# Attention into a gated feed-forward on one core: other SBUF places for TensorE's stationary operands

## The chip, the core and the metric

The kernel runs on one core of a Trainium2 chip. The time is that of the device for one execution, in microseconds (us); three runs of the kernel before gave 672.59 as their median (672.45 to 673.4).

## What is computed

Two attentions one after the other, and on their result a feed-forward with the gate h / (1 + exp(-1.702 h)):

```python
def sm_attn(qq, kk, vv):
    s = scale * np.matmul(qq, kk.transpose(0, 1, 3, 2))
    s = s - np.max(s, axis=-1, keepdims=True)
    a = np.exp(s)
    a = a / (np.sum(a, axis=-1, keepdims=True) + 1e-09)
    return np.matmul(a, vv)
p_packed = sm_attn(p, k, v)
out = sm_attn(q, p_packed, p_packed)
...
h = x @ w_in
g = h * (1.0 / (1.0 + np.exp(-1.702 * h)))
return (g @ w_out).astype(np.float32)
```

There are 8 batches, 8 heads, 576 positions, 64 numbers a head and 32 packed positions. x is the attention's output as 4,608 tokens of 512 numbers; w_in is 512 x 2048, w_out 2048 x 512. All is float32.

## The kernel before

**Stages.** The second attention is never multiplied out. Its probabilities a are kept, and the packed values times w_in give a matrix m for each batch and each 512 of the 2,048 inner columns (`m_mm`, L535); then h is m times a. Four steps carry nearly all of TensorE's time:

- `h_mm` (L687) makes 128 inner columns of h for 288 tokens with six matmuls. m is the stationary operand (128 columns), a the moving one (288 columns).
- `g_main`, `g_over`, `g_sum` (L716 to L769) take h through the gate on ScalarE and make sums of blocks of g on VectorE, for a product scheme with seven products of blocks. `g_upper` and `g_lower` (L776, L787) split the seven blocks into an upper and a lower part, the tile gs: 2 x 7 x 128 numbers a partition.
- `prod` (L851) is the product with w_out: a block of gs is stationary (128 columns), a block of Wa or Wb is moving (256 columns). Each of the seven products takes three matmuls (upper with upper, upper with lower, lower with upper), so a unit of 128 pairs of inner columns takes 21.
- `prod0` (L809) does the same for batch 0 without the scheme, with a moving operand of 512 columns.

Every matmul has a weight load of its own, which fetches the stationary operand. In the trace the weight load of the next matmul begins some 3 ns after the start of the matmul before it.

**What is where.** m, a, gs, Wa and Wb are tiles of the pool `wk` (L77). A pool gives each tag a stretch of SBUF, as many tiles as the tag has buffers, one after another in the order in which the tags are first used, each tile rounded up to a multiple of 32 bytes. There are four tiles each of Wa and Wb (`NU`, L70; tags by `kp % NU` in `w_tile`, L219), one for each of the four units u; so Wb3 serves all products of u = 3 with the Wb blocks, that is nine of the 21 matmuls of these units. The plain weights that are split into Wa and Wb lie in Wb's places first (`plain_w`, L226). All slices that the matmuls take begin at multiples of 128 bytes from their tile's start, so a tile's start modulo 128 is also that of its slices. In the program that is built these are:

| tile | role on TensorE | start modulo 128, before |
|---|---|---|
| gs (3 buffers, L781; one more in a place of m) | stationary | 0 (64 in m's place) |
| m (3, L565) | stationary | 64 |
| a (3, L657) | moving | 64 |
| Wa0 to Wa3 | moving | 64 |
| Wb0, Wb1, Wb2 | moving | 64 |
| Wb3 | moving | 0 |
| kqv, x (k, q, v, attention) | both | 64 |
| aT, PT | stationary | 0 |
| X, r, raw of w_out (aT's and r's places) | not read by TensorE | 0 |

**Order.** The order of all steps is written out by hand in the table `order` (L931 to L1731), and each engine runs its own instructions in that order. Two lines of it, with the products of one unit among the steps of another:

```python
        (prod, 1, 7, 0, 0, "C"), (g_lower, 1, 7, 0, 1), (h_mm, 1, 7, 1, 0, 0), (g_main, 1, 7, 0, 3),
        (g_lower, 1, 7, 0, 2), (g_over, 1, 7, 0, 3), (prod, 1, 7, 0, 1, "D"), (h_mm, 1, 7, 1, 0, 1),
```

Of the kernel before, what the change touches and what calls it, by code (L numbers as in the profile page):

```python
# [8 lines left out]
F32 = mybir.dt.float32  # L9
# [12 lines left out]
def kernel(  # L22
# [33 lines left out]
    P = 128  # L56
    D = P // 2
    DM, DF = w_in.shape
    NP = DM // P
    B = q.shape[0]  # L60
    S = q.shape[2] // NP
    NPK = pk.shape[2] // NP - S
    NH = S // 2
    G = S // NPK
    FC = 512
    HC = FC // 2
    CF = FC // P
    KC = (S + P - 1) // P
# [4 lines left out]
    ABUFS, XBUFS, GBUFS, RBUFS = 3, 3, 3, 2  # L73
# [3 lines left out]
    wk = ctx.enter_context(tc.tile_pool(name="wk", bufs=1))  # L77
    ps_acc = ctx.enter_context(tc.tile_pool(name="ps_acc", bufs=1, space=PSUM))
    ps_h = ctx.enter_context(tc.tile_pool(name="ps_h", bufs=2, space=PSUM))
    dram = ctx.enter_context(tc.tile_pool(name="dram", bufs=1, space=bass.MemoryType.DRAM))  # L80

    ident = cst.tile([P, P], F32, name="ident")
    make_identity(nc, ident)
# [84 lines left out]
    raw = {}  # L168
# [1604 lines left out]
```

## Time and profile before

| | us |
|---|---|
| median of three runs | 672.59 (672.45 to 673.4) |
| profiled execution, from its first to its last instruction | 672.0 |
| TensorE, matmuls | 658.8 |
| TensorE, weight loads | 598.2 |
| VectorE | 555.0 |
| ScalarE | 409.3 |

The page gives no time of the profiled execution other than that span. Busy times are unions of what an engine's instructions cover. A matmul's own duration holds its way through the array, and the next one starts before it ends; what a matmul costs in a dense stream is the time from its start to the next one's start. It can be read from the timeline: the rows there merge matmuls of one kind that follow each other, with the start of the first, and the start of the row below ends the stretch.

### The profile page before, as it was taken

The page shows a single profiled execution, that of the slowest core. Times are in us where ns is not written, and L with a number is a line of the kernel's source. Part 1 is how long each engine was busy: PE and PEld are TensorE (multiplying, and loading weights), DVE is VectorE, ACT ScalarE, POOL GpSimd, SP SyncE. Part 2 cuts the span into 40 slices and gives each one's busy share as a digit, 9 for nine tenths or more (in the row PEclk, how much of TensorE's full clock was granted, in tenths as well). Part 3 has the DMA queues.
Part 4 walks back from the last instruction along what each step waited for, and adds up shares of the span by engine and source line. Part 5 has one row for each costly group of instructions (what it writes and reads, how often), then busy time and mean ns, then how long its engine had stood idle before and what let it go on. Part 6 is the DMA issues. An engine that isn't in the chain of part 4 may idle for free.

```text
span 672.0 us, 15271 instructions
## 1 busy us (share of the span) xinstructions
PE 658.8 (98%) x6227; PEld 598.2 (89%) x6227; DVE 555.0 (83%) x1132; ACT 409.3 (61%) x738; POOL 5.4 (1%) x15
## 2 busy tenths in 40 slices
PE   8999899999999999999999999999999999999996
PEld 6777698988989899898999799999999999999996
DVE  3969988879799796987999846878898878886897
ACT  5878777858677695886978554444443544434441
POOL 2100000000000000000000000000000000000000
PEclk9999999999999999999999999999999999999999
DMA  9885646745465476463785315141252222233221
GB/s 342 306 283 182 228 95 222 200 166 217 110 243 144 163 232 188 156 182 137 259 292 187 128 36 155 54 173 50 82 180 88 87 88 87 62 112 87 87 88 63
DMA packets 59174, 104.92 MB, mean 156 GB/s; under 512 B 31392, under 2 KB 36128, under 8 KB 58208
## 3 DMA queue, kind: packets, MB, share of 16 engines
q1 hardware_dynamic: 58960, 103.81, 47.3%
q8 instruction: 49, 0.80, 0.5%
q14 instruction: 21, 0.17, 0.1%
q10 hardware_dynamic: 144, 0.13, 0.1%
HBM read 70.51 MB, written 33.42 MB: 155 GB/s over the span
## 4 chain that ended last, share of the span: by engine, by line
PE 79%; DMA 7%; DVE 7%; ACT 4%; SPq 2%; issue 1%; DVEq 0%; ACTq 0%
PE h L699 25%; PE accC L860 11%; PE accA L860 11%; PE accB L860 10%; PE accD L860 6%; PE psm_None L547 4%; DMA raw_in_None<-w_in 2%; PE accA_over L860 2%; PE accB_over L860 2%; DMA home_m<-w_in 1%; PE accC_over L860 1%; PE ps L591 1%; DMA aT<-aside 1%; PE pspv_None L496 1%; DMA home<-w_in 1%; PE accD L816 1%
## 5 line engine op out<-in xcount | busy, mean ns | idle before, releaser
L699 PE MATMUL h<-a,m 128*128 128x288 f32 x1536 | 223.8, 296 | 2.5 <-ACT x L111 1.3
L699 PEld LDWEIGHTS h<-a,m 128*128 128x128 f32 x1536 | 208.2, 188 | 8.2 <-ACT x L111 2.9
L111 ACT CAST gs<-X 128x896 fp32r<-128x896 f32 (+2 forms) x117 | 104.6, 902 | 75.8 <-DVE X L769 17.8
L789 DVE TENSOR_TENSOR gs<-X,gs 128x896 fp32r<-128x896 f32 x112 | 120.8, 1086 | 22.8 <-ACT gs L111 22.3
L719 ACT ACTIVATE X<-h 128x512 f32<-128x512 f32 (+1 forms) x129 | 76.1, 597 | 83.4 <-PE h L699 77.7
L769 DVE TENSOR_TENSOR X<-X 128x256 f32<-128x256 f32 (+1 forms) x336 | 104.6, 330 | 21.6 <-ACT X L719 17.2
L860 PE MATMUL accC<-Wa,gs 128*128 128x256 f32 x672 | 98.1, 281 | 0.0
L860 PE MATMUL accB<-Wb,gs 128*128 128x256 f32 x672 | 97.7, 281 | 0.0
L860 PEld LDWEIGHTS accC<-Wa,gs 128*128 128x128 f32 x672 | 87.3, 188 | 5.2 <-issue 4.3
L860 PEld LDWEIGHTS accB<-Wb,gs 128*128 128x128 f32 x672 | 87.3, 188 | 1.9 <-issue 0.9
L860 PE MATMUL accA<-Wa,gs 128*128 128x256 f32 x336 | 59.0, 284 | 0.0
L860 PE MATMUL accD<-Wa,gs 128*128 128x256 f32 x336 | 58.5, 282 | 0.0
L860 PE MATMUL accA<-Wb,gs 128*128 128x256 f32 x336 | 57.8, 280 | 0.0
L860 PEld LDWEIGHTS accA<-Wa,gs 128*128 128x128 f32 x336 | 47.7, 188 | 5.4 <-issue 5.1
L860 PEld LDWEIGHTS accD<-Wa,gs 128*128 128x128 f32 x336 | 48.0, 188 | 4.6 <-issue 2.2
L111 ACT CAST m<-psm_None 128x1024 fp32r<-128x1024 f32 x31 | 30.8, 1016 | 29.4 <-PE psm_None L547 29.0
L860 PEld LDWEIGHTS accA<-Wb,gs 128*128 128x128 f32 x336 | 47.5, 188 | 0.0
L571 DVE TENSOR_TENSOR m<-psm_None,m 128x1024 fp32r<-128x1024 f32 x31 | 37.3, 1217 | 6.7 <-ACT m L111 6.5
L725 ACT ACTIVATE over<-h 128x64 f32<-128x64 f32 x128 | 35.3, 289 | 0.0
L547 PE MATMUL psm_None<-w_in,PT 64*32 64x512 f32 x496 | 32.6, 596 | 0.8 <-DVE x L601 0.8
L665 DVE TENSOR_TENSOR a<-xt,a 128x576 fp32r<-128x576 f32 x31 | 23.1, 745 | 2.5 <-ACT a L111 2.1
L719 ACT ACT_TABLE_LOAD x17 | 21.8, 1283 | 4.3 <-PE h L699 3.0
(203 smaller groups left out, 794.4 us busy)
## 6 DMA issues: line engine op xcount, KB each, us to landing
part<-r SPq DMA_DIRECT2D x14, 896.0 KB, 5.4
p<-part SPq DMA_DIRECT2D x14, 896.0 KB, 5.5
q<-q SPq DMA_DIRECT2D x16, 576.0 KB, 5.4
o<-r SPq DMA_DIRECT2D x16, 512.0 KB, 3.5
raw_out_None<-w_out SPq DMA_DIRECT2D x16, 511.8 KB, 5.6
v<-v SPq DMA_DIRECT2D x7, 1024.0 KB, 5.6
raw_in_None<-w_in SPq DMA_DIRECT2D x12, 511.8 KB, 4.8
k<-pk SPq DMA_DIRECT2D x8, 640.0 KB, 4.0
```

Of the source, the lines that this page charges most:

```text
L111: nc.scalar.copy(dst, src)
L496: nc.tensor.matmul(bank[32 * j : 32 * j + 32, e, e * D : (e + 1) * D], turned()[:, c, e, 32 * j : 32 * j + 32], vt[:, c, e0 : e0 + D], sta ...
L547: nc.tensor.matmul(banks[eo][32 * j : 32 * j + 32], PT[rows(eo), j, :], w_in_sb[c % 2][rows(eo), j, at], start=True, stop=True,)
L571: nc.vector.tensor_tensor(m[:, 1, :, at], st["bank", "m", b, c, part], m[:, 0, :, at].bitcast(F32), op=ALU.subtract,)
L591: nc.tensor.matmul(bank[32 * j : 32 * j + 32, eo, :NH], st["PT", b][rows(eo), j, :], kq["q0", half][rows(eo), j, :] if b == 0 else kq["q", ...
L665: engine.tensor_tensor(even_odd(a[:, 1], eo), even_odd(st["t", 2, b, half], eo), even_odd(a[:, 0], eo).bitcast(F32), op=ALU.subtract,)
L699: nc.tensor.matmul(h, m[:, part, eo, at], a[:, ap, eo * NH : (eo + 1) * NH], start=(n == 0), stop=(n == len(terms) - 1), skip_group_check= ...
L719: nc.scalar.activation(X[:, :4].rearrange("p (f t) n -> p f (t n)", f=2)[:, chunks(f)], st["h", *k][:, chunks(f), :NM], AF.Gelu_apprx_sigm ...
L725: nc.scalar.activation(over_part(ph, b, half, u), st["h", ph, b, half, u][:, :, NM:NH], AF.Gelu_apprx_sigmoid, scale=2.0,)
L769: engine.tensor_tensor(to, a, b_, op=ALU.subtract)
L789: engine.tensor_tensor(lo, X, hi.bitcast(F32), op=ALU.subtract)
L860: nc.tensor.matmul(acc[:, n * HC : (n + 1) * HC], gs[:, gp, g], Wa[:, wp, w] if w < 4 else Wb[:, wp, w - 4], start=(u == 0 and n == 0 and ...
```

## The change

At the pool's start a tile of each of the pool's tags is made, in a new order of the tags, with four tags that nothing else uses (`pad1` to `pad4`, of 32 or 96 bytes). No instruction touches these tiles; the kernel's own tiles then take the same stretches. Each engine's instructions, their order and the semaphores that they wait for and set are the same as before. Only addresses differ.

```diff
     dram = ctx.enter_context(tc.tile_pool(name="dram", bufs=1, space=bass.MemoryType.DRAM))
+
+    places = (
+        ("mx1", 2, 2), ("nb1", 2, 2), ("sm1", 2, 2), ("again", 1, 2), ("rs1", 1, 4), ("rsa", 1, 2),
+        ("mx2", G, 2), ("sm2", G, 2), ("rs2", G, 2),
+        ("kqv", KC * DM, 2), ("x", S, 6), ("Wb2", 6 * HC, 1), ("pad1", 8, 1),
+        ("gs", 14 * P, GBUFS), ("pad2", 24, 1), ("aT", KC * 2 * P, 1), ("X", 8 * P, XBUFS),
+        ("r", 7 * HC, 2), ("pn", 2 * D, 1), ("PT", P, 8), ("Wb3", 6 * HC, 1), ("raw", 2 * FC, RBUFS),
+        ("Wb0", 6 * HC, 1), ("pad3", 8, 1), ("m", 4 * FC, 3), ("pad4", 24, 1),
+    )
+    for tag, words, bufs in places:
+        for i in range(bufs if words else 0):
+            wk.tile([P, words], F32, tag=tag, name=f"place_{tag}_{i}", bufs=bufs)
 
     ident = cst.tile([P, P], F32, name="ident")
```

The starts that result, modulo 128:

| tile | before | changed |
|---|---|---|
| gs | 0 (64 in m's place) | 96 (also in m's place) |
| m | 64 | 96 |
| a, Wa0 to Wa3, Wb0 to Wb2, kqv, x | 64 | 64 |
| Wb3 | 0 | 64 |
| aT, PT, X, r | 0 | 64 |

The first weights of w_in, which are loaded into places of gs and of m at the program's start (`raw_tile`, L174), move with these.

## Rows read from the trace of the kernel before

**Rows 1.** The page: its first line, and busy time by engine (share, instructions).

```profile
span 672.0 us, 15271 instructions
PE 658.8 (98%) x6227; PEld 598.2 (89%) x6227; DVE 555.0 (83%) x1132; ACT 409.3 (61%) x738; POOL 5.4 (1%) x15
```

**Rows 2.** The page: granted TensorE clock in 40 slices, tenths of full speed.

```profile
PEclk9999999999999999999999999999999999999999
```

**Rows 3.** The page: chain that ended last, share of the span by engine.

```profile
PE 79%; DMA 7%; DVE 7%; ACT 4%; SPq 2%; issue 1%; DVEq 0%; ACTq 0%
```

**Rows 4.** Waits of TensorE, longest: us in total, times, longest us.

```profile
PE accD_warm L119 <- POOL ident masks.py:199: 1.4, 1, 1.4
```

**Rows 5.** Costly groups: line engine op, shapes, count | busy us, mean ns | idle before.

```profile
L699 PE MATMUL h<-a,m 128*128 128x288 f32 x1536 | 223.8, 296 | 2.5 <-ACT x L111 1.3 <-ACT over L725 1.0
...
L860 PE MATMUL accC<-Wa,gs 128*128 128x256 f32 x672 | 98.1, 281 | 0.0
...
L816 PE MATMUL accC<-Wa,gs 128*128 128x512 f32 x48 | 13.1, 404 | 0.0
...
L860 PE MATMUL accA_over<-Wb,gs_over 128*128 128x256 f32 x48 | 8.2, 280 | 0.0
```

**Rows 6.** Windows: length, each engine's busy us (count), PEclk, DMA share, GB/s.

```profile
415.07:419.15 4.08, 4.08 (x37) 4.08 (x36) 3.56 (x9) 2.66 (x5) 0.00 (x0) 1.00 0.96 308
257.23:262.05 4.82, 4.82 (x43) 4.82 (x42) 1.75 (x7) 1.51 (x3) 0.00 (x0) 1.00 0.74 274
```

**Rows 7.** Timeline of TensorE from 415.07: start us, us covered, operation, count.

```profile
415.07 0.50 PE L860 MATMUL accD<-Wa,gs 128*128 128x256 f32 x3
...
419.15 0.43 PE L699 MATMUL h<-a,m 128*128 128x288 f32 x2
```

**Rows 8.** Timeline of TensorE from 257.23, first and last start taken.

```profile
257.23 0.87 PE L860 MATMUL accC<-Wa,gs 128*128 128x256 f32 x6
...
261.82 0.51 PE L860 MATMUL accD<-Wa,gs 128*128 128x256 f32 x3
```

**Rows 9.** Timeline of TensorE: two stretches of nine products with Wb3, then what follows.

```profile
356.15 0.53 PE L860 MATMUL accA<-Wb,gs 128*128 128x256 f32 x3
...
357.24 0.52 PE L860 MATMUL accC<-Wa,gs 128*128 128x256 f32 x3
...
287.16 0.52 PE L860 MATMUL accA<-Wb,gs 128*128 128x256 f32 x3
...
288.23 0.56 PE L699 MATMUL h<-a,m 128*128 128x288 f32 x3
```

**Rows 10.** Timeline of TensorE: three long stretches of h, and what follows each.

```profile
591.17 4.91 PE L699 MATMUL h<-a,m 128*128 128x288 f32 x36
595.92 0.52 PE L860 MATMUL accB<-Wb,gs 128*128 128x256 f32 x3
...
322.57 3.29 PE L699 MATMUL h<-a,m 128*128 128x288 f32 x24
325.69 0.40 PE L860 MATMUL accD<-Wa,gs 128*128 128x256 f32 x2
...
580.49 3.39 PE L699 MATMUL h<-a,m 128*128 128x288 f32 x24
583.71 0.51 PE L860 MATMUL accD<-Wa,gs 128*128 128x256 f32 x3
```

**Rows 11.** Two of VectorE's lines: durations ns min/median/max, first and last start us.

```profile
L276 DVE TENSOR_TENSOR T<-E x16: 416/418/426, 57.3 to 376.2; 128x256 f32<-128x256 f32 x16
...
L789 DVE TENSOR_TENSOR gs<-X,gs x112: 1030/1086/1095, 81.7 to 651.0; 128x896 fp32r<-128x896 f32 x112
```

**Rows 12.** DMA issues into places of gs and of m: KB each, median us to landing.

```profile
home<-w_in SPq DMA_DIRECT2D x4, 255.8 KB, 7.5
home_m<-w_in SPq DMA_DIRECT2D x4, 255.8 KB, 6.7
```

## The prediction

> **What bounds the kernel now.** I read the page's head first. TensorE's matmuls cover 658.8 of the 672.0 us, VectorE follows with 555.0 and ScalarE with 409.3 [rows 1]. The granted clock is 9 tenths or more in every slice, the higher of its two levels (2.4 GHz), so no stretch is long because of the clock [rows 2]. The chain of waits that ended last runs for 79% on TensorE, with 7% each for DMA and VectorE [rows 3]. TensorE's own longest wait is 1.4 us, before the first matmul [rows 4]. So after the start-up the time is the number of matmuls times their pitch, the time from one start to the next, and the only thing that the change can do to the end is to alter that pitch, or to make another engine so slow that TensorE waits.
>
> The costly groups give the numbers [rows 5]: 1,536 matmuls of 288 columns (h, stationary m, moving a); 2,688 of 256 columns in ten groups (the products, stationary gs, moving Wa or Wb; the first and the last group are shown); 192 of 512 columns in four groups (first shown). The durations in these rows overlap (the next weight load runs during each matmul), so I don't use them. The pitch comes from the timeline.
>
> Two stretches show that the pitch isn't fixed. From 415.07 us, 36 products in a row take 4.08 us: 113.3 ns each [rows 7]. From 257.23 us, 39 products in nine rows take 4.59 us: 117.7 ns [rows 8]. Both have gs at 0 and Wa or Wb at 64 modulo 128 bytes. The windows tell that the load of the other engines isn't the reason: the **faster** stretch has VectorE busy 3.56 of 4.08 us and the DMA engines at 0.96, the slower one 1.75 of 4.82 and 0.74 [rows 6]. So one and the same pair of places has two pitches, and what the slow one pays, 4.4 ns a matmul, looks like something that happens between the two reads of TensorE itself: the weight load of the next matmul and the moving operand of this one.
>
> The places do matter, but less. Before the change one buffer breaks the pattern: Wb3 lies at 0, where gs also lies. Nine products with it take 1.09 us from 356.15 (121.1 ns), nine 1.07 us from 287.16 (118.9 ns) [rows 9]: 120.0 on the mean, 2.3 more than 117.7. For h, both operands lie at 64, also a distance of 0. Its stretches stand at 131.9, 130.0 and 134.2 ns [rows 10].
>
> **The change part by part.** Instructions, order and waits stay; only distances change. The distance from the moving to the stationary operand, modulo 128, becomes 32 for all three kinds. It was 64 for 2,400 of the products and for the 192 wide matmuls, 0 for the 288 products with Wb3 (9 in each of 32 units) and 0 for h.
>
> 1. Products with Wb3, 288: the distance 0 goes. I take the pitch of the other products: 288 x (120.0 - 117.7) = -0.7 us. Bounds: 0 if the place had no part in it; -1.9 us at 113.3 (288 x 6.7).
>
> 2. h, 1,536: the distance 0 goes too. No stretch shows h at another distance. The bounds are its own extremes: from 131.9 down to 130.0 is -2.9 us, up to 134.2 is +3.5 us. I take half of the way down, -0.95 ns, which is under half of the 2.3 ns that the products show between the distances 0 and 64: -1.5 us. I don't take all 2.3, because h shows no surplus over the products: its 32 more columns cost 131.9 - 117.7 = 14.2 ns, and 32 columns at 117.7 / 256 ns would be 14.7.
>
> 3. Products at 64, 2,400: to 32. This is the largest number and the one that the trace shows least. Bounds: all at 113.3 is -10.6 us; all at the slowest stretch with Wb3, 121.1, is +8.2 us. I take 0: long stretches at different buffers and different times sit at 117.7, so the slow pitch is a stable state that arises at most starts, and nothing in the rows says that 32 leaves it. The 192 wide ones I cost at 0 as well, for the same reason; at 4.4 ns either way they are 0.8 us.
>
> 4. The writers of the moved tiles. VectorE's sums of 256 elements take 416 to 426 ns with a median of 418 over tiles at 0 and at 64 [rows 11], so these two places cost it the same; 96 isn't shown. If each of the 112 lower parts of g (1,086 ns) [rows 11] grew by as much as that row's spread, 10 ns, VectorE would have 1.1 us more in a span where it idles 117 us. I cost it at nothing; TensorE's stream is the cover, and if it were gone the bound is that 1.1 us. The transfers into the gs places took 7.5 us at 0, into the m places 6.7 us at 64 [rows 12]; these wait in queues behind one another, so I read no effect of the place from the difference. They matter in the first 30 us only: 0, with 0.8 us either way.
>
> Sum: -0.7 - 1.5 = -2.2 us on a span of 672.0, so 669.8. The median of the runs, 672.59, is 0.6 us above that span (the page gives no other time for its execution), so the forecast is 670.4 us.
>
> The rows show two pitches at equal places [rows 7, 8] and a third, 2.3 ns longer, at another place [rows 9]. Against the whole change stands a rule of the Trainium skill: TensorE: Matmul & The Clock Gate, in Step-by-step: what each phase is for, says that TensorE reads SBUF through two independent ports and that loading the next weights takes no read bandwidth from the running matmul; by it the sum is 0 and the time stays 672.6. The equal places agree with it in so far as the place isn't all, the 2.3 ns speak against it. The same page, in Back-to-back issue gap, gives columns / 2.4 + 2.5 ns for an isolated matmul, 109.2 for 256 columns (an estimate from its formula); no stretch here gets there, the best is 113.3.
>
> **The rivals.** *The fast pitch becomes the rule.* If the distance 32 keeps the two reads from meeting, all products go to 113.3: 10.6 + 1.9 us. h would go to 113.3 + 14.2 = 127.5, another 1,536 x 4.4 = 6.8 us, and the wide ones 0.8: 20.1 us. VectorE would then be close behind in its dense stretches, so I keep three quarters: 15 us, 657 us. For it: the state exists, for 36 products on end and under more load. Against it: no row has the distance 32, and the state is rare.
>
> *The new distance is worse.* The reads meet more often, as they seem to with Wb3. If all products go to 121.1 and h to 134.2, that is 8.2 + 0.3 + 3.5 = +12.0 us, 684.6; half-way, 678.6. It decides as soon as the 2,400 products lose 0.9 ns on the mean, which eats the 2.2 us of steps 1 and 2. For it: a pitch at one distance tells nothing of that at another, and one distance was shown to be worse. Against: the distance that is worse is removed everywhere.
>
> *Nothing happens.* The pitch is set by how the stream starts after a wait, and Wb3's 2.3 ns come from something else, since the stretch at 287.16 pays only half as much. h without a surplus at the distance 0 speaks for it too (step 2). Then 672.6. The page TensorE: Matmul & The Clock Gate of the Trainium skill would have it so, by the rule above.
>
> **How the numbers follow.** Forecast 0.35, fast pitch 0.27, worse distance 0.23, nothing 0.15. About 0.2% (1.3 us) is what a measurement here can tell from no change. The forecast is beyond it by 0.9 us only, so a seventh of its chance (0.05) counts as the same: faster 0.30 + 0.27 = 0.57, same 0.05 + 0.15 = 0.20, slower 0.23. For the range, the lower end takes in the fast pitch to 656, which leaves out some 0.08 in which nearly all of the 20.1 us arrive; the upper end takes in the worse distance to just over its half-way point, 679, and leaves out some 0.10. The likeliest case's own range is 668.5 to 672.
>
> **What would show it.** In the changed kernel's timeline: nine products with Wb3 in 1.06 us (step 1); long runs of h nearer to 131 than to 132 ns (step 2); products of the other buffers at 117.7 ns (step 3); the groups of VectorE and ScalarE with unchanged means and still no wait of TensorE above 2 us (step 4). The forecast is wrong if the products' stretches stand at another pitch than 117.7: at 113 to 115 the first rival holds, at 119 or more the second. If Wb3 still shows 119 to 121 at its new place, the reason for step 1 was wrong.

## The result and the profile after

The changed kernel takes 676.15 us (median of four runs, 675.55 to 677.19) beside 672.52 for the kernel before (672.03 to 673.4): 1.0055 times the time, 95% interval 1.0042 to 1.0067. It is slower by 3.6 us, where 2.2 us less was forecast. The time lies inside the range, on the wrong side of no change.

The page of the changed kernel: first line, busy time, granted clock, shares of the chain that ended last ([rows 1 to 3] of before). Lines of the code behind the insertion have moved by 12.

```profile
span 673.8 us, 15271 instructions
PE 661.1 (98%) x6227; PEld 600.6 (89%) x6227; DVE 555.4 (82%) x1132; ACT 409.8 (61%) x738; POOL 5.4 (1%) x15
PEclk9999999999999999999999999999999999999999
PE 82%; DVE 6%; ACT 5%; DMA 4%; SPq 1%; issue 1%; DVEq 0%; ACTq 0%
```

The instructions are as many as before, the clock stayed at its higher level, VectorE and ScalarE gained 0.4 and 0.5 us of busy time, and TensorE's matmuls 2.3. So it is the pitch of the matmuls. The two profiled executions differ by 1.8 us only, because of which ones they were. A run's time lies some 1.8 us above its span wherever both are known (675.6 and 673.8 us here), so the span of 672.0 before belongs to an execution of about 673.8 us (an estimate), 1.2 above the median, while the changed kernel's was one of its two quickest. The start-up was 0.6 us shorter too (VectorE's L801 starts first at 81.1 us, in [rows 11] at 81.7); from there to the end it is 592.7 against 590.3 us.

The stretches of [rows 7, 8, 9] in the changed kernel's timeline, with the same matmuls: start us, us covered, operation, count.

```profile
415.55 0.52 PE L872 MATMUL accD<-Wa,gs 128*128 128x256 f32 x3
...
419.80 0.29 PE L711 MATMUL h<-a,m 128*128 128x288 f32 x1
```
```profile
257.08 0.87 PE L872 MATMUL accC<-Wa,gs 128*128 128x256 f32 x6
...
261.70 0.28 PE L872 MATMUL accD<-Wa,gs 128*128 128x256 f32 x1
```
```profile
356.36 0.51 PE L872 MATMUL accA<-Wb,gs 128*128 128x256 f32 x3
...
357.43 0.28 PE L872 MATMUL accC<-Wa,gs 128*128 128x256 f32 x1
```

36 products take 4.25 us, 118.1 ns each (113.3 before); 39 take 4.62 us, 118.5 (117.7); nine with Wb3 take 1.07 us, 118.9 (121.1). The long run at 113.3 is gone. The three stretches of h ([rows 10]), and the row behind each:

```profile
592.66 4.95 PE L711 MATMUL h<-a,m 128*128 128x288 f32 x36
597.45 0.28 PE L872 MATMUL accB<-Wb,gs 128*128 128x256 f32 x1
```
```profile
322.60 3.35 PE L711 MATMUL h<-a,m 128*128 128x288 f32 x24
325.78 0.28 PE L872 MATMUL accD<-Wa,gs 128*128 128x256 f32 x1
```
```profile
582.00 3.36 PE L711 MATMUL h<-a,m 128*128 128x288 f32 x24
585.20 0.28 PE L872 MATMUL accD<-Wa,gs 128*128 128x256 f32 x1
```

That is 133.1, 132.5 and 133.3 ns against 131.9, 130.0 and 134.2. The other engines are as before. First the windows of the two long stretches of products (VectorE busy 3.62 and 1.79 us, in [rows 6] 3.56 and 1.75), then VectorE's line of [rows 11] with the moved tile as its output, min/median/max:

```profile
415.55:419.80 4.25, 4.25 (x37) 4.25 (x36) 3.62 (x9) 2.63 (x5) 0.00 (x0) 1.00 0.95 306
257.08:261.70 4.62, 4.62 (x41) 4.62 (x40) 1.79 (x7) 1.29 (x3) 0.00 (x0) 1.00 0.66 244
```
```profile
L801 DVE TENSOR_TENSOR gs<-X,gs x112: 1027/1085/1094, 81.1 to 652.6; 128x896 fp32r<-128x896 f32 x112
```

A few stretches are samples, so I also took the time from start to start of each matmul to the next of its kind right behind it, over the whole trace (some 2,500 pairs of products, 1,400 of h, 165 of the 512-column ones). Sorted by the distance **modulo 256** bytes from the moving start to the stationary start of the next matmul, the means are:

| ns | before | changed |
|---|---|---|
| products, most buffers | 117.7 at 192; Wb2 116.5 at 64 | 118.2 at 32 |
| products with Wb3 | 119.3 at 0 | 119.2 at 160 |
| products with Wb0 | 117.6 at 192 | 119.3 at 160 |
| all products | 117.72 | 118.46 |
| h | 132.26, at 0 and 128 | 132.87, at 32 and 160 |
| 512 columns | 231.2 at 192 | 232.9 at 32 |

(h changes between two distances because its moving slices lie 1,152 bytes apart, which is 128 modulo 256.) 0.74 x 2,688 + 0.61 x 1,536 + 1.74 x 192 ns = 2.0 + 0.9 + 0.3 = 3.3 us (from the unrounded terms) of the 3.6. That the distance causes this, and modulo 256, is what the experiments are for.

### The profile page after: what moved, and what is told of

It reads as the page before. It is cut to its first block, busy times and chain, and to the rows that moved or that the text cites. A ratio compares the mean times of both kernels' runs of the same rounds, so it can differ in the third digit from the quotient of the medians.

```text
span 673.8 us, 15271 instructions
## 1 busy us (share of the span) xinstructions
PE 661.1 (98%) x6227; PEld 600.6 (89%) x6227; DVE 555.4 (82%) x1132; ACT 409.8 (61%) x738; POOL 5.4 (1%) x15
## 4 chain that ended last, share of the span: by engine, by line
PE 82%; DVE 6%; ACT 5%; DMA 4%; SPq 1%; issue 1%; DVEq 0%; ACTq 0%
PE h L711 26%; PE accC L872 11%; PE accA L872 11%; PE accB L872 11%; PE accD L872 6%; PE psm_None L559 4%; PE accA_over L872 2%; PE accB_over L872 2%; PE accC_over L872 1%; DMA home_m<-w_in 1%; DMA home<-w_in 1%; PE ps L603 1%; PE pspv_None L508 1%; PE accD L828 1%; ACT L731 1%
## 5 line engine op out<-in xcount | busy, mean ns | idle before, releaser
L801 DVE TENSOR_TENSOR gs<-X,gs 128x896 fp32r<-128x896 f32 x112 | 120.8, 1086 | 23.4 <-ACT gs L123 22.8
```

The costliest lines, as they stand in the source:

```text
L801: engine.tensor_tensor(lo, X, hi.bitcast(F32), op=ALU.subtract)
```

## The experiments

**1. The pitch by itself.** A kernel that holds nothing of the computation but bursts of 24 matmuls. Until 43 us the transfers that write its zeros run beside them (DMA share 1.04 from 33.0 to 36.2 us); after that nothing does. The letters a to p are distances 0 to 240 in steps of 16 bytes; the moving operand starts at 192 modulo 256. The loop, with its names' values put in:

```python
for i in range(24):
    m, s = i % 4 * 256, 4 * letter + i % 7 * 128
    nc.tensor.matmul(t[:, :256], sta[:, s : s + 128], mov[:, m : m + 256], start=True, stop=True)
```

> This kernel leaves out the whole computation and writes zeros: it only streams matmuls, 24 in a burst, with one burst for each distance from the moving to the stationary operand in steps of 16 bytes (letters a to p: 0 to 240), moving operand at 64 modulo 128. 'prod' has 256 columns, 'wide' 288, each twice, after one and after two other matmuls; 'other' has 256 columns with the moving operand at 0 modulo 128 (letter a is then the distance -64, e is 0). Theory distance: the pitch is a function of the distance modulo 128, the same after both starts; from the two kernels, 256 columns: about 119.5 ns at 0 (a, i), 118.5 at 32 (c, k), 117.7 at 64 (e, m), and somewhere another distance at 113; 288 columns about 132 at 0 and 133 at 32. 'other' then repeats the row of 'prod', shifted by four letters. Theory start: the pitch is a state that the stream falls into when it starts; the two bursts of one letter differ as much as those of different letters (113 to 121), and no distance stands out. Theory place: the moving operand's own place sets it; then all letters of 'prod' are equal, near 117.7, and all of 'other' are near 120.

Timeline, bursts c (32), e (64) and m (192), the last two at both of their starts, in order of time:

```profile
27.15 3.09 PE L51 MATMUL prod_c<-mov,sta 128*128 128x256 f32 x24
...
33.27 2.99 PE L51 MATMUL prod_e<-mov,sta 128*128 128x256 f32 x24
...
57.73 2.97 PE L51 MATMUL prod_m<-mov,sta 128*128 128x256 f32 x24
...
83.22 3.08 PE L51 MATMUL prod_e<-mov,sta 128*128 128x256 f32 x24
...
109.58 3.07 PE L51 MATMUL prod_m<-mov,sta 128*128 128x256 f32 x24
```

A burst's 0.10 us over 23 steps is 4.3 ns a step. Over each burst without its first three steps: 118.4 and 118.0 ns at 32; 113.8 and 117.8 at 64; 113.35 and 117.8 at 192; 119.8 at 0 (its second burst; during the first the granted clock was 0.74); 116.6 to 120.1 at the rest. So with no other engine computing the distance alone moves the pitch by 6 to 7 ns, the change's 32 isn't a fast one, and 64 and 192 hold either of two pitches: the choice is made at the start of a burst. The transfers don't make it: the fast burst at 64 ran under them, the slow one and both at 192 didn't. With the moving operand 64 bytes further (16 more bursts) the fast burst was again the one at distance 64 (113.5 ns), so it is the distance, not the place. Bursts of 288 columns, the size of h's, lay between 131.9 and 133.6, so there is no fast pitch for h; with the distances of before (0 and 128 in turn) they took 132.7 to 132.9, with those of the change (32 and 160) 133.1 to 133.5.

**2 to 4. The same move with other pads.** From here to experiment 7 only the words of the four pads differ from the changed kernel's; the cuts show the pads' entries alone. gs and m at 0 modulo 128 (e2):

```diff
-("pad1", 8, 1), ("pad2", 24, 1), ("pad3", 8, 1), ("pad4", 24, 1),
+("pad1", 16, 1), ("pad2", 16, 1), ("pad3", 16, 1), ("pad4", 16, 1),
```

> The change with gs and m at 0 instead of 96; moving operands at 64, Wb3 too, so the distance is 64 modulo 128 for every product and for h. Theory distance: products at 117.7 ns on the mean, those with Wb3 too, h at or under the 132.2 of before: 670 to 672 us, 4 to 6 us under the changed kernel. Theory start: anywhere between 668 and 678 us with pitches that differ from buffer to buffer. Theory that the move of X, r, aT, PT and Wb3 to 64 costs the time (they move here too): as the changed kernel, 676 us.

At 64 (e3):

```diff
-("pad1", 8, 1), ("pad2", 24, 1), ("pad3", 8, 1), ("pad4", 24, 1),
+("pad1", 0, 1), ("pad2", 0, 1), ("pad3", 0, 1), ("pad4", 0, 1),
```

> The change with gs and m at 64, moving operands at 64: distance 0 for every product and for h. Theory distance: products at 119.5 to 120 ns, h at 132.2 as before: 2,688 x 1.8 to 2.3 ns = 5 to 6 us over the kernel before, 677 to 679 us. Theory start: no relation, 668 to 678 us. Theory of the other tiles: 676 us.

At 32 (e4):

```diff
-("pad1", 8, 1), ("pad2", 24, 1), ("pad3", 8, 1), ("pad4", 24, 1),
+("pad1", 24, 1), ("pad2", 8, 1), ("pad3", 24, 1), ("pad4", 8, 1),
```

> The change with gs and m at 32, moving operands at 64: distance 96 modulo 128. Theory distance: a distance not seen so far; if only its size counts, as at 32: products at 118.5, h at 132.9, 676 us. If the sign counts (which of the two reads is ahead), another value, 668 to 680 us. Theory of the other tiles: 676 us.

Distance 64 (e2): 667.72 us, 0.9927 (0.9913 to 0.994). Distance 0 (e3): 676.9 us, 1.0062 (1.0049 to 1.0074). Distance 96 (e4): 673.77 us, 1.0018 (1.0008 to 1.0028). The 36 products of [rows 7] in e3:

```profile
416.04 0.52 PE L872 MATMUL accD<-Wa,gs 128*128 128x256 f32 x3
...
420.36 0.30 PE L711 MATMUL h<-a,m 128*128 128x288 f32 x1
```

and the 39 of [rows 8] in e2:

```profile
256.71 0.84 PE L872 MATMUL accC<-Wa,gs 128*128 128x256 f32 x6
...
261.16 0.28 PE L872 MATMUL accD<-Wa,gs 128*128 128x256 f32 x1
```

4.32 us for 36 are 120.0 ns each in e3; 4.45 us for 39 are 114.1 in e2. The instructions, their order and the rest of the engines are the same in all of them, so the places alone are worth 9 us here. Modulo 128 only gs and m differ between e2 and e3; modulo 256 Wb0 and Wb3 do too. In e2 the products with Wb0 and Wb3 stayed at 117.9: modulo 256 they are at 192, the others at 64 (114.5). Modulo 128 these are the same place. e2 ended 2 us below what was expected, since the expectation knew of no fast pitch at 64.

**5. gs moved alone, m left where it was (both modulo 128).**

```diff
-("pad3", 8, 1), ("pad4", 24, 1),
+("pad3", 0, 1), ("pad4", 0, 1),
```

> The change with only gs at 96 (distance 32 for the products), m left at 64 (distance 0 for h, as before). Theory distance: products as in the changed kernel (118.5 ns), h as before (132.3 instead of 132.9): the changed kernel less 1,536 x 0.6 = 0.9 us, 675.2 us. If h's place carries the loss instead, 672.5; if the interplay of both, 676.

676.82 us, 1.0063 (1.0051 to 1.0076), 1.6 us above the expectation. h is back at 132.31 ns, as before the change (132.26), so the 0.6 ns of h came with m's place. This is the weaker of the readings: over the seven kernels with m and a as before, h lies between 132.0 (e6) and 132.5 ns (e11), a spread nearly as large; the changed kernel and e4, at 132.9, lie above it. The products are at 119.7, worse than in the change, since modulo 256 the pads' sum moved other tiles as well: here Wa and three of the Wb buffers lie at 160 and only one at 32.

**6, 7. All moving buffers of the products at one place modulo 256** (192), gs at 128 (distance 192) and at 0 (distance 64); m and a as before:

```diff
-("pad1", 8, 1), ("pad2", 24, 1), ("pad3", 8, 1), ("pad4", 24, 1),
+("pad1", 48, 1), ("pad2", 16, 1), ("pad3", 0, 1), ("pad4", 0, 1),
```

> gs at 128 and all of Wa and Wb at 192 modulo 256, m and a as in the kernel before: every product has the distance -64 (192 modulo 256), which is what Wa and two of the Wb had before; Wb3 differs from before in its place alone. Theory that 256 is the period: products at 117.7, fast pitch rare; only the 288 products with Wb3 gain (119.3 to 117.7, 0.5 us): 671.5 to 672 us. Theory that 128 is the period: the same as the kernel with all at 0, where more than half of the products have the fast pitch: 667 to 668 us.

```diff
-("pad1", 8, 1), ("pad2", 24, 1), ("pad3", 8, 1), ("pad4", 24, 1),
+("pad1", 16, 1), ("pad2", 48, 1), ("pad3", 0, 1), ("pad4", 0, 1),
```

> gs at 0 and all of Wa and Wb at 192 modulo 256: every product has the distance +64; m and a as in the kernel before (distance 0 for h). Theory that 256 is the period: the products with Wb0 and Wb3, 117.9 ns in the kernel with all at 0, go to 114.5 like the others: 540 x 3.4 = 1.8 us, and h gains 1,536 x 0.3 = 0.5 us on that kernel's 132.6: 665.4 us. Theory that 128 is the period: as the kernel with all at 0, less 0.5 us for h: 667.2 us.

e6: 671.51 us, 0.9983 (0.9974 to 0.9992). This is step 1 of the prediction done alone and with the right period: the nine products with Wb3 of [rows 9],

```profile
355.41 0.52 PE L872 MATMUL accA<-Wb,gs 128*128 128x256 f32 x3
355.76 0.87 PE L872 MATMUL accB<-Wb,gs 128*128 128x256 f32 x6
356.47 0.28 PE L872 MATMUL accC<-Wa,gs 128*128 128x256 f32 x1
```

take 1.06 us, 117.8 ns each, and over the trace Wb3's mean is 117.7 in place of 119.3. e7: 668.7 us, 0.994 (0.9927 to 0.9953), with Wb0 and Wb3 at 115.6 and 116.0 like the rest. The 36 products of [rows 7], all at 64 here, are in the fast pitch:

```profile
412.22 0.51 PE L872 MATMUL accD<-Wa,gs 128*128 128x256 f32 x3
...
416.31 0.57 PE L711 MATMUL h<-a,m 128*128 128x288 f32 x3
```

That is 4.09 us, 113.6 ns each. Nearly all products are at 64 now, but their mean is 115.8, no better than e2's 115.2: more buffers have the distance, and less of the time at it is fast. I had expected 665.4; the expectation took the fast pitch for granted.

**8, 9. Finer steps, other widths, and the kernel's own order of addresses.** e8 has bursts as in 1, with steps of 4 bytes around 64 and with 288 and 512 columns; e9 runs the addresses of two units of products and of one `h_mm`, in the kernel's order, at each distance from 0 to 252 in steps of 4 bytes. Neither computes anything else. The loop of e9, in short:

```python
for i in range(64):
    lead(1)
    for s, m in unit * 2:
        nc.tensor.matmul(t[:, :256], sta[:, i + s : i + s + P], mov[:, m : m + 256], start=True, stop=True)
```

> Leaves out the whole computation and writes zeros; streams of matmuls alone. 'wide': 288 columns, 16 distances in steps of 16 bytes, the moving blocks now 1,280 bytes apart, so that the distance modulo 256 stays the same within a burst (before it went up and down by 128 as in the kernel). Theory distance with period 256: one letter has a fast pitch near 127.5 ns, 32 x 0.44 over 113.3, as e and m had at 256 columns; else all stay at 132 to 134 and no place helps h. 'fine': 256 columns at distances of 52 to 76 bytes in steps of 4 (d is 64): if the fast pitch needs exactly 64, only d has it; if it needs the same line of 16 or 32 bytes, d to g have it. 'full': 512 columns, 16 distances: the best near 226 ns at 0 (a), the others 229 to 234.

> Leaves out the whole computation and writes zeros; streams of matmuls alone, with the kernel's own order of addresses: 42 products of two units, 256 columns, then 24 matmuls of h, 288 columns, for each distance from 0 to 252 bytes in steps of 4 (letters aa to hh, the second letter the faster: aa 0, bb 36, cc 72). Theory distance: 'prod' near 120 at 0 (aa), 118 to 119.5 at 32 (ba), 113 to 118 at 64 (ca), 117.7 at 192 (ga), 117 to 118 at 224 (ha); fast pitches at single words near 64 bytes, 12 bytes apart, as at 52, 64 and 76 before; 'wide' 132.3 at 0, 132.9 at 32, and between 131 and 134 everywhere, so that no place gives h more than 1.3 ns. Theory start: no relation to the kernels' means.

e8, distances 64, 68 and 76 (one start of each):

```profile
142.37 2.98 PE L50 MATMUL fine_d<-mov,sta 128*128 128x256 f32 x24
145.33 3.08 PE L50 MATMUL fine_e<-mov,sta 128*128 128x256 f32 x24
...
151.44 2.97 PE L50 MATMUL fine_g<-mov,sta 128*128 128x256 f32 x24
```

e9, distances 64, 68, 72 and 76, 42 products each:

```profile
105.49 5.03 PE L51 MATMUL prod_ca<-mov,sta 128*128 128x256 f32 x42
...
110.49 5.21 PE L51 MATMUL prod_cb<-mov,sta 128*128 128x256 f32 x42
...
115.68 5.22 PE L51 MATMUL prod_cc<-mov,sta 128*128 128x256 f32 x42
...
120.88 5.01 PE L51 MATMUL prod_cd<-mov,sta 128*128 128x256 f32 x42
```

Four bytes decide: 113.3 ns at 64, 118.4 at 68, 118.2 at 72, 113.3 at 76. e8 adds that 52 is fast as well and 56 and 60 aren't (117.8 and 119.6 ns), so neither expectation on 'fine' came true. Its 'wide' bursts lay between 131.2 and 133.5 ns with no fast one, and its 'full' ones were quickest at 16, 144 and 240 (226.7 ns), not at 0 (228.9), and took up to 234.1. Over all 64 distances of e9 the pitch 113.3 is reached at five: 52, 64, 76, 88 and 180 (in 72, 90, 100, 88 and 80% of the steps); the rest lie at 115.9 to 121.5. h lies at 131.5 to 134.9 everywhere, best at 88, 112 and 124. The map against what the whole kernels did:

| distance | e9, products | kernels, products |
|---|---|---|
| 0 (second half of the burst; granted clock 0.56 in the first) | 119.7 | before 119.3, e3 119.5 |
| 32 | 118.2 | changed 118.2 |
| 64 | 113.3 in 90% of the steps (e1 also 117.8) | before 116.5, e2 114.5, e7 115.7 |
| 96 | 117.35 | e4 117.9 |
| 160 | 119.8 | changed 119.2 |
| 192 | 117.75 (e1 also 113.35) | before 117.7, e2 117.9, e6 117.7 |
| 224 | 116.7 | e4 117.2 |

That 256 bytes is the period also shows where distances differ by just that: in the changed kernel the products at 32 and at 288 bytes modulo 512 take 118.28 and 118.24 ns.

**10, 11. 76 and 68 bytes in the kernel.** gs in three tags of one buffer, taken in the order in which the kernel before takes its three buffers; each slice begins `GOFF` words into its tile, and the places put the tile's start 64 above the moving ones modulo 256:

```diff
+        return wk.tile([P, 14 * P + 8], dtype, tag="gs" + SLOTS[made[0] - 1], name=name)
...
+                t = gs_tile(name, F32R)
+            st["gs", k] = t[:, GOFF : GOFF + 14 * P].rearrange("p (i n e) -> p i n e", i=2, n=7)
```

`GOFF` is 3 in e10 and 1 in e11.

> What runs: the kernel before with gs in places whose slices begin 76 bytes after those of all moving operands of the products, modulo 256 (three tags in place of three buffers, the slots taken in the order of the kernel before; m, a and Wa, Wb0 to Wb2 keep their residues, Wb3 joins them). Theory D (the distance between stationary and moving start, to 4 bytes and modulo 256, sets the pitch, and some distances hold two pitches of which the neighbours pick one): the map e9 held 113.3 ns in all of its steps at 76, from the first one, where 64 held it in 90%. So the products of 256 columns (2,530 of the kernel's matmuls stand in this distance) take 113.3 to 113.8 in place of 117.7: -10.6 us; the 512-column products have no row at 76, 233.4 at 64 in e8 against 231.2 before: +0.4; h stays at 132.3. Total 662.3 us, 660.5 to 664. Rival S (what costs the fast pitch in the kernel is not the distance but the writers and the changes between kinds of matmuls, which the micro runs lack): the share of fast products stays near the half of e7, 115.8 ns, 668.7 us. Rival N (the map is of the micro stream alone): 117 to 118.5, 670 to 675.

> What runs: the same with 68 bytes in place of 76. Theory D: e8 showed 118.35 ns at 68, between two fast distances, so the products take 118.2 to 118.5 in place of 117.7: +1.6 us, P0 +0.4, total 674.5 (673 to 676), 12 us more than the run with 76 for a shift of 8 bytes. Rival S: near the 668.7 of the run with 64, since 4 bytes are little. Rival T (what made e2 and e7 faster is that gs was moved into other places, not the distance): both runs give the same time.

e11: 674.41 us, 1.0029 (1.0016 to 1.0042), products at 118.37 ns: theory D to the digit (674.5 us, 118.2 to 118.5). The 36 products of [rows 7] in e11 take 4.26 us, 118.3 ns each:

```profile
414.80 0.52 PE L881 MATMUL accD<-Wa,gs 128*128 128x256 f32 x3
...
419.06 0.29 PE L720 MATMUL h<-a,m 128*128 128x288 f32 x1
```

e10: 668.53 us, 0.9939 (0.9924 to 0.9955), 115.74 ns where theory D expected 113.3 to 113.8; here rival S was right (668.7 us, 115.8 ns). Eight bytes are worth 6 us, so S's "4 bytes are little" and T are out; but the distance alone doesn't give the fast pitch, and S's other half, that something in the whole kernel keeps many stretches from it, stands; which of the two things that S named it is, or another, isn't shown. The timeline of e10 shows what the miss consists of. Two long stretches, each with its end (start us, us covered, operation, count):

```profile
354.39 0.50 PE L881 MATMUL accD_over<-Wa,gs_over 128*128 128x256 f32 x3
354.73 0.84 PE L881 MATMUL accB_over<-Wb,gs_over 128*128 128x256 f32 x6
...
363.23 0.43 PE L720 MATMUL h<-a,m 128*128 128x288 f32 x2
```
```profile
577.73 0.52 PE L881 MATMUL accD<-Wa,gs 128*128 128x256 f32 x3
578.09 0.88 PE L881 MATMUL accC<-Wa,gs 128*128 128x256 f32 x6
...
585.29 0.43 PE L720 MATMUL h<-a,m 128*128 128x288 f32 x2
```

78 products in 8.84 us are 113.3 ns each, 63 in 7.56 us are 120.0, with the same kinds of tile at the same distance. A stretch takes one of the pitches within some seven steps of its start and, with few exceptions, keeps it to its end. Of the 76 stretches with nine steps or more in e10, 59 end at 113 to 114 ns (1,584 steps, 115.8 on the mean in their first seven) and 17 stay near 120 (616 steps). 616 x 6.6 + 59 x 7 x 2.5 + 304 steps in shorter stretches x 3.0 = 4.1 + 1.0 + 0.9 = 6.0 us, which is the miss of 6.2. In e7 (64), 46 of 75 end fast. In the kernel before it is 1 of 73, in e6 (192) 3 of 74, in the changed kernel and in e3, e4, e5 and e11 none. In e2, where Wb0 and Wb3 lie at 192 among buffers at 64, 29 of the 44 stretches of twenty steps or more change their pitch on the way. How a start chooses isn't settled: all long stretches from 577 to 612 us in e10 chose 120 and most before chose 113, with h between them each time.

The three best kernels, e2 (667.72 us), e10 (668.53) and e7 (668.7), beat both the kernel before and the changed one; their intervals overlap, so none is shown to be the best. Put together, the pitches account for every kernel's median to 1.7 us or better (mean pitch against before, times 2,688, 1,536 and 192). The pitches come from one profiled execution of each kernel, though, and against the spans of these, of which that of before was a long one, the agreement is to 3.1 us:

| us against before | change | e2 | e3 | e4 | e5 | e6 | e7 | e10 | e11 |
|---|---|---|---|---|---|---|---|---|---|
| by the pitches | +3.3 | -5.8 | +4.3 | +1.6 | +5.9 | -0.6 | -4.6 | -5.0 | +2.4 |
| measured (ratio) | +3.7 | -4.9 | +4.2 | +1.2 | +4.2 | -1.1 | -4.0 | -4.1 | +2.0 |
| span of the profiled execution, less 672.0 | +1.8 | -3.5 | +3.4 | -0.5 | +2.8 | -1.0 | -4.7 | -5.5 | +0.6 |

## Why the prediction was wrong

**What bounds the kernel** held: no engine became late, TensorE's longest wait is still 1.4 us, and the difference is pitch, 3.3 of the 3.6 us by the sum above.

**Steps 3 and 2 failed, and together they turned the sign.** Between the -2.2 us of the forecast's sum and the +3.3 us that the pitches give, step 2 (h) is 2.4 us, step 3 (the 2,400 products) 2.0, step 1 0.7 and the wide products 0.3. With step 3 alone wrong, the time would have come out about equal.

**Step 3** costed the 2,400 products at 0 because "nothing in the rows says that 32 leaves it", the slow pitch. There is not one slow pitch: each distance has its own, and 32 costs 118.2 where 192 cost 117.7. Beneath it lies the period. The prediction counted distance modulo 128, so it took Wa, Wb0, Wb1 and Wb2 to lie alike; but 64 and 192 differ by 3 ns (e2), and only modulo 256 do the buffers of one pitch fall together. Before, most of them were at 192, and Wb2 at 64, where the means are lower (116.5); afterwards Wb0 went to 160, at 119.3, as dear as Wb3 had been. Of the 2.0 us, Wb0 and Wb2 are 0.5 each and the other buffers 1.0. The two pitches of [rows 7] and [rows 8] were real, as the prediction said: every one of the 36 products of [rows 7] stands at 192, where e1 and e6 have both pitches too. But the fast stretch was the only one of the 73 long ones, and nothing in those rows could tell which distances allow it.

**Step 1** (-0.7 us for Wb3) gave nothing: 119.3 before, 119.2 after. By the prediction's own sign, Wb3 at 119 to 121 in its new place, the reason for step 1 would be wrong. It was half right: distance 0 is dear (e3, 119.5), but the new distance is 160 and not 32, and as dear. With the right place (e6) Wb3 got the 117.7 that step 1 asked for. Its price was too high as well: two stretches gave 120.0 before the change, the whole trace 119.3, so that the full gain is 0.5 us.

**Step 2** (-0.95 ns for h) had the wrong sign: +0.6 ns, +0.9 us. The guess took half the way to h's own quickest stretch, in the direction in which the products gain from 0 to 64. In e9 h costs 132.1 at 0 and 131.6 at 128, where it was, and 132.45 and 132.8 at 32 and 160, where it went. The spread between its stretches in [rows 10] wasn't one of distance: 130.0 and 134.2 stood at the same mix of places, and the three stretches now lie within 0.8 ns.

**The 192 wide products**, costed at 0 within 0.8 us, took 0.3 us more. **Step 4** was right: VectorE's L801 has a median of 1085 ns against 1086, and TensorE's waits for it are 0.2 us in all.

**The rivals.** "The new distance is worse" is what happened, at 3.6 of the 6.0 us of its half-way point: it needed 0.9 ns on the products to decide against gains of 2.2 us, and with those gains absent 0.74 sufficed. "The fast pitch becomes the rule" named something real, a pitch of 113.3 that a place can give, but 32 isn't such a place; at 64 and 76 it is, for about half to three quarters of the steps, and -15 us was too much, as h has no share in it. "Nothing happens" had the pitch set by how the stream starts. That is half of what the runs show: at 64, 76 and 192 a start does choose between two pitches, but which pitches there are is a matter of the distance. The rule that it cited from the Trainium skill (TensorE: Matmul & The Clock Gate, Step-by-step: what each phase is for) is that TensorE has two independent read ports and that loading the next weights takes no read bandwidth from the running matmul. The runs speak against what the prediction drew from it, that the places cost nothing: with only the stationary start moved, by 8 bytes, e10 and e11 differ by 6 us, and e9's pitch goes from 113.3 to 121.5 ns. The formula of that page's Back-to-back issue gap, by which 256 columns take 109.2 ns (an estimate), was reached in no run.

## What to carry to other kernels

Where TensorE runs dense with a new stationary operand for each matmul, the two operands' start addresses are part of the cost: here up to 6% of a product's pitch, by their distance modulo 256, to 4 bytes. Don't reason about a new distance from an old one; a kernel of a few microseconds per distance, with the real widths and address order, gives the price of each, and its map told the whole kernels' pitches to 0.6 ns wherever the distance had a single pitch. Look for a distance that is fast from the first step, count on getting some half of its gain where the stream is broken up (e10 got 5.3 of 10.6 us on its products), and check every buffer of the moving operand modulo the full period.

## What the runs showed of the hardware beyond that

- One and the same stream at one distance has two stable pitches, 113.3 and 117.8 ns at 64 and 192, 113.3 and 120.0 at 76; the stretch settles within about seven matmuls and mostly stays.
- Neighbouring fast distances lie 12 bytes apart (52, 64, 76, 88), with 117.5 to 119.9 ns between them; 180 stands alone.
- The widths answer differently: in the whole kernels 512 columns were quickest at distance 0 (228.9 ns in e3 against 231.2 at 192 and 234.1 at 96), where 256 columns are near their slowest. 288 columns moved by at most 3.4 ns in e9 and showed no fast pitch.
- Whether the two reads collide, and in what, isn't shown by any record; why just these distances are fast, and how a start chooses its pitch, stays open.
